# A gated mix of dilated local attention and a feed-forward layer: where the second parity's pipeline of logits and mixes begins

## The chip, the cores and the metric

The kernel runs on one core of a Trainium2 chip. The metric is the device time of one execution in microseconds; a profiled execution also has a span, from its first to its last instruction.

## The reference

Two layers share the input `x` (2048 tokens of 512 channels, float32) and are mixed by a gate per token:

```python
qkv = x @ wqkv                                  # 32 heads of 16 channels
idx = pos[:, None] - 2 * arange(8)[None, :]     # 8 keys, two tokens apart, back in time
logits = einsum(q, k[idx]) * 16 ** -0.5         # -1e9 where idx < 0
a = einsum(softmax(logits), v[idx]) @ wo
b = (gelu(x @ w_gate) * (x @ w_up)) @ w_down    # 1792 hidden channels
g = sigmoid((x * gate_w).sum(-1, keepdims=True))
return g * a + (1 - g) * b
```

A token looks only at tokens of its own parity, so even and odd tokens are two independent halves.

## The kernel before, in words

The two halves ("parities", 0 and 1) are worked one after the other. For each parity TensorE makes keys and queries (`keys`, and two last products in `key_one`), then values and the gate (`values`), and then the feed-forward layer in `ffn(par)`: 14 groups `f` of 128 hidden channels, each with seven products of gate and up weights (`gate_up`, L781 in `product`) and, from `f` = 2 on, pieces of the down projection (`down`, L830). All matrix products are split in a high and a low half of each operand and summed (three matmuls for one), and the gate, up and value products are combined from sums and differences of blocks, so that seven block products do the work of eight. VectorE and ScalarE make the sums, the halves (the low half of a hidden block is L801), the GELU and the copies out of the accumulators. The halves of the weights come partly from memory again (`ws`) and partly through an accumulating DMA of GpSimd (L740).

Attention runs beside that on VectorE. It is cut in eight *units*, four per parity (128 channels, so 8 heads, each). For a unit there are:

- `load_kq`: three DMAs on SyncE's queue for keys (L523, L524) and queries (L520) into a tile `kq` that exists once.
- `scores` (the logits): four times a product of 128 x 2048 elements (L539) and a sum over the 16 channels of a head (L542), and a mask for the first tokens (L546).
- `exps`: maximum (L553) and subtraction (L555) on VectorE, exponential on ScalarE (L557, with a load of the function's table ahead of it).
- `shares`: sum (L562), reciprocal (L564), for the second parity the product with the gate (L566), and the product with the exponentials (L568).
- `load_values`: two DMAs (L523, L524) into a tile `v` that exists once.
- `mix`: four times a product (L585) and three halving sums (L589, L591, L593), and after every second of them a transposition (L598) and four DMAs on SyncE's queue that store it (L600, `os`).

The logits of a unit live in one of two tiles `lg`; the product of L539 and of L585 goes to one tile `prod`.

A generator, `attention`, writes these steps in one order. The code of the matrix products calls `pull` with a budget at many places; each step of the generator has a price, and as many steps are emitted there as the budget buys. L539 and L585 (`paced`) are also tied to the last matmul emitted by then, and so can't start before it. All steps are emitted at a lower priority than the work around them. A planner with a simulated timeline then lays down each engine's own order; VectorE, ScalarE, SyncE and GpSimd work theirs in that order. At the very end `need_o` emits what is left of a unit before `finish` reads its stored result (L1040), halves it (L90, L91) and multiplies it with `wo` (L1062).

The loop of the generator over the units, `i` from 0 to 7 (unit 4 is the second parity's first), cut to what the change touches:

```python
            if i not in ready:
                if i >= PIPE and keyed(i + 1):
                    load_kq(*units[i + 1])
                yield from exps(*un)
            ...
            pipe, ahead = i >= PIPE and keyed(i + 1), i and keyed(i + 1)
            if not pipe and ahead:
                load_kq(*units[i + 1])
            load_values(*un)
            if pipe:
                yield from logits(i + 1)
                ...
                yield from exps(*units[i + 1])
            ...
            yield from mix(*un)
            ...
            elif ahead:
                yield from logits(i + 1)
```

`keyed(i)` says that the keys and queries of unit `i` have been emitted; `logits` is `scores`, with `load_kq` ahead of it if that wasn't done yet. With `pipe`, the shares of unit `i + 1` follow the mix of unit `i`.

Of the kernel before, what the change touches and what calls it, by code (L numbers as in the profile page):

```python
# [33 lines left out]
LOAD = 4.0  # L34


PIPE = 4
BT = 4
MASKED = -1e9 * DH ** 0.5
LOWS = (4, 8, 10), (4, 6, 8, 10, 12)  # L40
# [8 lines left out]
def tile_gated_mix(ctx: ExitStack, tc: tile.TileContext, xt, wqkv, wff, wo, out):  # L49
# [458 lines left out]
    def load_kq(par, u):  # L508
        hh, c = divmod(u, 2)
        kq = KQ.pop() if KQ else pool.tile([P, 3 * NP - 1, UC], F32, name="kq")  # L510
        k, q = kq[:, :2 * NP - 1], kq[:, 2 * NP - 1:]
        LG[par, u] = k, q
        if not (par or u):

            nc.gpsimd.memset(k[:1, :NP - 1], 0.0)
            for a, b in (1, P - 15), (P - 15, P):
                nc.sync.dma_start(k[a:b, :NP - 1], k[a - 1:b - 1, NP:])
            return
        load_slots(k, KS[par, hh][c], paced)
        paced(nc.sync.dma_start(q, QS[par, hh][c].rearrange("(p j) d -> p j d", j=NP)))  # L520
# [38 lines left out]
    def shares(par, u):  # L559
        lg = LG[par, u]  # L560
        m = pool.tile([P, UH, NP], F32, name="m")
        nc.vector.tensor_reduce(m, lg, axis=AX.X, op=OP.add)  # L562
        yield 0.7
        nc.vector.reciprocal(m, m)  # L564
        if par:
            nc.vector.tensor_tensor(m, m, g[:, par, None, :].to_broadcast([P, UH, NP]), op=OP.mult)  # L566
        yield 0.4
        nc.vector.tensor_tensor(lg, lg, m[:, :, :, None].to_broadcast([P, UH, NP, W]), op=OP.mult)  # L568
        yield 0.7
# [52 lines left out]
    def attention():  # L622
# [3 lines left out]
        def keyed(i):  # L626
            return i < len(units) and (units[i][0], units[i][1] // 2 * 2) in done
# [12 lines left out]
        for i, un in enumerate(units):  # L640
# [4 lines left out]
# [4 lines that stand above are left out]
            yield from need(un[0], 1)  # L649
            if i not in shared:  # L650
                yield from shares(*un)
            pipe, ahead = i >= PIPE and keyed(i + 1), i and keyed(i + 1)
            if not pipe and ahead:
# [702 lines left out]
```

## Time and profile before

| | |
|---|---|
| median of 3 runs | 593.22 us (592.76 to 597.3) |
| profiled execution | 592.89 us, span 591.1 us |
| TensorE busy | 585.7 us (99% of the span), clock 1.00 |
| VectorE busy | 535.0 us (91%) |
| ScalarE busy | 425.3 us (72%) |
| GpSimd busy | 126.8 us (21%) |
| HBM, over the span | 197 GB/s |

Busy time of an engine is the time in which one of its instructions ran. In the groups of instructions, a row gives line, engine, operation, what is written and read, and how often; in the timeline a row gives start and length in microseconds, and in brackets how long the engine sat idle before it and what ended that. In the list of waits a row gives the total, the count and the longest. A name with q behind the engine (SPq) is its queue of DMA issues. The second parity's keys are made from about 276 us on, its values follow, and its feed-forward runs from about 330 to 533 us.

### The profile page before, as it was taken

Reading aid. Unit: us, or ns where it says so; the run is one execution under the profiler, and the core shown is the slowest. Engines: PE = TensorE matmul, PEld = TensorE weight load, DVE = VectorE, ACT = ScalarE, POOL = GpSimd, SP = SyncE. Lnnn points to the kernel's source line nnn. Section 1 sums busy time; section 2 is a strip of 40 time slices with the busy share of each in tenths; the row PEclk is TensorE's granted clock in tenths of the full one; section 3 lists DMA queues with packets and bytes.
Section 4 is the critical chain, followed back from the end, with each engine's and each line's share of the span. In section 5 each row is a group of like instructions: output and inputs, shape, how many; then the busy total and the mean of one; then the engine's idle time right before and its main releaser. Section 6 shows DMA issues by size and latency. Waiting matters only on the chain.

```text
span 591.1 us, 8266 instructions
## 1 busy us (share of the span) xinstructions
PE 585.7 (99%) x2743; PEld 489.1 (83%) x2743; DVE 535.0 (91%) x628; ACT 425.3 (72%) x752; POOL 126.8 (21%) x153
## 2 busy tenths in 40 slices
PE   9999999999999999999999999999999999999997
PEld 7889888888888888888889888888888888887885
DVE  6989998999899995998997999998999899989882
ACT  6778667778887779786687655768776967796522
POOL 0140751112111212113120761112121212112200
PEclk9999999999999999999999999999999999999999
DMA  8789999978987979899989999969798989548915
GB/s 305 228 247 281 301 310 231 296 197 238 289 222 218 273 205 273 224 264 347 284 231 380 222 272 269 277 162 257 178 263 224 254 213 247 144 111 227 202 44 178
DMA packets 87848, 141.71 MB, mean 240 GB/s; under 512 B 8575, under 2 KB 49919, under 8 KB 87806
## 3 DMA queue, kind: packets, MB, share of 16 engines
q1 hardware_dynamic: 65454, 103.21, 52.2%
q0 software_dynamic: 22064, 37.59, 34.6%
q8 instruction: 21, 0.34, 0.2%
q10 hardware_dynamic: 288, 0.39, 0.2%
q14 instruction: 21, 0.17, 0.1%
HBM read 69.83 MB, written 46.49 MB: 197 GB/s over the span
## 4 chain that ended last, share of the span: by engine, by line
PE 96%; ACT 2%; DMA 1%; issue 0%; SPq 0%; DVE 0%; ACTq 0%
PE p L781 44%; PE p L830 13%; PE acc L830 12%; PE acc L478 11%; PE p L1062 6%; PE p L364 4%; PE acc L364 3%; PE p L478 2%; PE acc L1062 2%; DMA raw<-xt 1%; ACT A L90 0%; ACT L898 0%; ACT g L135 0%; ACT hl L805 0%; ACT hh L807 0%
## 5 line engine op out<-in xcount | busy, mean ns | idle before, releaser
L781 PE MATMUL p<-S,g 128*128 128x512 f32 x672 | 167.0, 389 | 0.0
L781 PEld LDWEIGHTS p<-S,g 128*128 128x128 f32 x672 | 125.8, 188 | 25.8
L781 PE MATMUL p<-A,g 128*128 128x512 f32 x504 | 125.8, 389 | 0.0
L781 PEld LDWEIGHTS p<-A,g 128*128 128x128 f32 x504 | 94.4, 188 | 19.8 <-ACT rt L845 0.4
L585 DVE TENSOR_TENSOR prod<-v,lg 128x2048 f32<-128x2048 f32 x32 | 72.8, 2274 | 1.4 <-DMA v<-vs 1.2
L542 DVE TENSOR_REDUCE lg<-prod 128x128 f32<-128x2048 f32 x32 | 73.0, 2280 | 0.2
L539 DVE TENSOR_TENSOR prod<-kq 128x2048 f32<-128x2048 f32 x32 | 72.9, 2277 | 0.2
L830 PE MATMUL p<-d,hh 128*128 128x512 f32 x224 | 68.6, 390 | 0.3 <-ACT p L824 0.3
L830 PE MATMUL acc<-d,hh 128*128 128x512 f32 x224 | 59.7, 389 | 0.0
L740 POOL DMA_DIRECT2D g<-raw x26 | 23.6, 907 | 161.1 <-ACT g L737 103.6
L792 ACT ACTIVATE c<-p 128x512 f32<-128x512 f32 x56 | 33.4, 597 | 33.7 <-PE p L781 33.6
L830 PEld LDWEIGHTS p<-d,hh 128*128 128x128 f32 x224 | 41.9, 188 | 9.5 <-ACT p L824 0.8
L830 PEld LDWEIGHTS acc<-d,hh 128*128 128x128 f32 x224 | 42.0, 188 | 8.7
L793 DVE TENSOR_TENSOR c<-c,s 128x512 f32<-128x512 f32 x56 | 37.8, 681 | 5.5 <-ACT c L792 5.2
L830 PE MATMUL p<-d,hl 128*128 128x512 f32 x112 | 42.1, 389 | 0.0
L797 DVE TENSOR_TENSOR c<-c 128x512 f32<-128x512 f32 x56 | 38.1, 683 | 1.3 <-ACT c L898 1.2
L589 DVE TENSOR_TENSOR prod<-prod 128x1024 f32<-128x1024 f32 x32 | 39.0, 1217 | 0.1
L845 ACT ACTIVATE rt<-p 128x512 f32<-128x512 f32 x48 | 27.8, 596 | 15.0 <-PE p L830 14.8
L786 ACT ACTIVATE s<-p 128x512 f32<-128x512 f32 x56 | 33.2, 594 | 5.3 <-PE p L781 4.9
L478 PE MATMUL acc<-d,S 128*128 128x512 f32 x144 | 35.5, 390 | 0.1
L830 PE MATMUL acc<-d,hl 128*128 128x512 f32 x112 | 35.1, 389 | 0.0
L772 POOL DMA_DIRECT2D d<-r x23 | 19.8, 860 | 68.9 <-ACT d L771 41.6
(222 smaller groups left out, 1062.3 us busy)
## 6 DMA issues: line engine op xcount, KB each, us to landing
g<-raw POOLq DMA_DIRECT2D x26, 512.0 KB, 6.7
ws<-g SPq DMA_DIRECT2D x14, 768.0 KB, 5.9
g<-ws SPq DMA_DIRECT2D x14, 768.0 KB, 6.7
r<-wff SPq DMA_DIRECT2D x28, 256.0 KB, 4.4
raw<-wff SPq DMA_DIRECT2D x14, 512.0 KB, 4.6
d<-r POOLq DMA_DIRECT2D x23, 256.0 KB, 6.7
ws<-raw SPq DMA_DIRECT2D x14, 384.0 KB, 5.8
raw<-ws SPq DMA_DIRECT2D x14, 384.0 KB, 4.0
```

The costliest lines, as they stand in the source:

```text
L364: LAST[:] = [nc.tensor.matmul(ps[:, :n], x[:, ts], VO[b][w][:, kc * WQ:kc * WQ + n], start=first, stop=(kc == 1 and i == 2), skip_group_ch ...
L478: LAST[:] = [nc.tensor.matmul(ps, x[:, ts], w, start=(start and kc == i == 0), stop=(kc == 1 and i == 2), skip_group_check=True)]
L539: paced(nc.vector.tensor_tensor(prod, spans(k, jj), q[:, jj:jj + 2, None, :].to_broadcast([P, 2, W, UC]), op=OP.mult))
L542: nc.vector.tensor_reduce(two_of(lg, jj), prod.rearrange("p j w (h d) -> p (j w) h d", d=DH), axis=AX.X, op=OP.add)
L585: paced(nc.vector.tensor_tensor(prod.rearrange("p j w (h d) -> p (j w) h d", d=DH), spans(v, jj).rearrange("p j w (h d) -> p j w h d", d=D ...
L589: nc.vector.tensor_tensor(prod[:, :, :4], prod[:, :, :4], prod[:, :, 4:], op=OP.add)
L781: LAST[:] = [nc.tensor.matmul(ps, w_, a_, start=(start and kc == 0 and n == 0), stop=(kc == 1 and n == 2), skip_group_check=True)]
L792: nc.scalar.activation(c, ps, AF.Copy)
L793: nc.vector.tensor_tensor(c, c, s, op=OP.add)
L797: nc.vector.tensor_tensor(ge, ge, up, op=OP.mult)
L830: LAST[:] = [nc.tensor.matmul(pp, a[:, ts], w, start=(i == 0 and n == 0 and gr == 0), stop=(i == 1 and n == 2), skip_group_check=True)]
L1062: LAST[:] = [nc.tensor.matmul(pa, a, b, start=(first and n == 0), stop=(last and n == 2), skip_group_check=True)]
```

## The change

One constant goes from 4 to 5. It is read at the two places quoted above only.

```diff
-PIPE = 4
+PIPE = 5
```

For units 5 and later nothing changes in the generator. For unit 4 the condition `i >= PIPE` is now false. So its `exps` are not preceded by `load_kq` of unit 5; that load follows unit 4's `shares`, ahead of `load_values`. The logits and the exponentials of unit 5 no longer stand between unit 4's shares and its mix: the mix comes first, then unit 5's logits. Unit 6's keys and queries are loaded, and unit 5's exponentials and shares emitted, at the head of the next turn of the loop. The order of steps goes from

logits 4, exps 4, shares 4, logits 5, exps 5, mix 4, shares 5, logits 6, ...

to

logits 4, exps 4, shares 4, mix 4, logits 5, exps 5, shares 5, logits 6, ...

and the steps from logits 6 on stand as before.

## The prediction

> **What bounds the kernel now.** I read the head of the page first, then what TensorE waits for, then what VectorE waits for, and last the timelines of VectorE, SyncE and ScalarE in the stretch that the edit reorders.
>
> ```profile
> span 591.1 us, 8266 instructions
> PE 585.7 (99%) x2743; PEld 489.1 (83%) x2743; DVE 535.0 (91%) x628; ACT 425.3 (72%) x752; POOL 126.8 (21%) x153
> PEclk9999999999999999999999999999999999999999
> PE 96%; ACT 2%; DMA 1%; issue 0%; SPq 0%; DVE 0%; ACTq 0%
> PE p L76 <- DVE warm L73: 1.0, 1, 1.0
> PE p L830 <- ACT p L824: 0.3, 1, 0.3
> DVE m L562 <- ACT lg L557: 15.3, 7, 4.1
> DVE c L793 <- ACT c L792: 5.2, 8, 1.4
> DVE prod L585 <- DMA v<-vs: 1.2, 1, 1.2
> ```
>
> TensorE is busy for 585.7 of 591.1 us at the full granted clock, is 96% of the chain that ended last, and waits for nothing but 1.0 us at the start and 0.3 us once. Nearly all of the 5.4 us in which it is idle is lead-in and the tail behind the last matmul. So a reordering of attention work on VectorE can hardly gain: at most the 0.3 us, and nothing of the matmuls, whose number stays the same. It can lose as soon as it makes TensorE wait. The question is therefore how much slack each of VectorE's products for TensorE has, and what the edit takes from it.
>
> **The stretch that is reordered.** Write S for a unit's logits (L539 and L542, four pairs), E for its exponentials (L553, L555 on VectorE, then L557 on ScalarE), H for its shares (L562 to L568), M for its mix (L585 to L598), and number the units 0 to 7; unit 4 is the second parity's first. These rows of the timeline (start, length, engine, line) are what the present order S4 E4 (H4) S5 (E5) M4 (H5) S6 leaves:
>
> ```profile
> 342.33 0.38 SPq L523 DMA_DIRECT2D v<-vs  x1
> 367.01 2.29 DVE L539 TENSOR_TENSOR prod<-kq 128x2048 f32<-128x2048 f32 x1
> 369.32 0.32 SPq L523 DMA_DIRECT2D kq<-ks  x1
> 376.28 0.68 DVE L555 TENSOR_TENSOR lg<-lg,m 128x512 f32<-128x512 f32 x1
> 376.50 1.28 ACT L557 ACT_TABLE_LOAD   x1
> 376.88 2.29 DVE L539 TENSOR_TENSOR prod<-kq 128x2048 f32<-128x2048 f32 x1
> 377.79 0.63 ACT L557 ACTIVATE lg<-lg 128x512 f32<-128x512 f32 x1
> 379.08 0.68 DVE L562 TENSOR_REDUCE m<-lg 128x64 f32<-128x512 f32 x1
> 382.47 0.55 DVE L564 RECIPROCAL m<-m 128x64 f32<-128x64 f32 x1
> 386.28 0.22 DVE L566 TENSOR_TENSOR m<-m,g 128x64 f32<-128x64 f32 x1
> 389.21 0.68 DVE L568 TENSOR_TENSOR lg<-lg,m 128x512 f32<-128x512 f32 x1
> 399.68 0.33 SPq L523 DMA_DIRECT2D kq<-ks  x1
> 403.67 2.27 DVE L585 TENSOR_TENSOR prod<-v,lg 128x2048 f32<-128x2048 f32 x1
> 411.55 0.69 DVE L562 TENSOR_REDUCE m<-lg 128x64 f32<-128x512 f32 x1 [2.22 <-ACT lg L557]
> 421.30 3.81 SPq L600 DMA_DIRECT2D os<-tb  x4
> 430.19 0.82 SPq L523 DMA_DIRECT2D v<-vs  x1
> 433.72 2.25 DVE L539 TENSOR_TENSOR prod<-kq 128x2048 f32<-128x2048 f32 x1
> 433.83 2.93 SPq L600 DMA_DIRECT2D os<-tb  x4
> ```
>
> The reader is to see three things. First, between L555 of unit 4 (ends 376.96) and L562 (379.08) stands the first logits instruction of unit 5: it covers unit 4's exponential. Unit 5's exponential, met within unit 4's mix, is not covered: L562 waits 2.22 us. Second, unit 4's values were already requested at 342.33, at once when unit 3's mix had read its last, and 61 us before the mix that uses them: loads go out when their buffer is free, not where the source puts them. Third, unit 5's keys go out at 369.32, when unit 4's last L539 ends, and the first S5 runs at 376.88 with no wait.
>
> **The change part by part.** No instruction, byte or matmul is added or removed. The order becomes S4 E4 H4 M4 S5 E5 H5 S6, and from S6 on it is the old one. Both orders spend the same budget ahead of S6, so the matmuls to which S6 and all later work are tied are the same.
>
> *Unit 4's exponential loses its cover.* The mix needs the shares, so nothing of the attention can stand between L555 and L562. Exposed: 377.79 + 0.63 = 378.42, minus 376.96, is 1.46 us of idle VectorE. Bounds: 0, if the product work of the feed-forward (0.6 us apiece) fills it, and 4.1, the longest such wait in the waits above. I take 1.5, as this very exponential was timed.
>
> The Trainium skill, "ScalarE: Activation LUTs", section "What ACT_TABLE_LOAD costs", charges a switch of tables with 1.28 us of load and a further 1.38 us of drain. The load has that length here, but the exponential starts at 377.79, 0.01 us behind it, so the second part does not appear behind the load; by the page's full figure this exposure would be an estimated 2.8 us in place of 1.5.
>
> *Unit 5's exponential gains a cover.* Unit 6's first logits now follow H5, as unit 5's followed H4, so the 2.22 us wait goes in full if unit 6's keys are there. Bounds: −2.2 to 0. I take −2.2, from the like case at 376.88.
>
> *The mix comes earlier, its values are there.* Unit 4's shares come out at about 378.4 + 0.68 + 0.55 + 0.22 + 0.68 = 380.6, and up to 2 us later with feed-forward work between. The values were asked for 38 us before that (342.33). Cost 0; the load of unit 5's values moves from 430.19 to about 410, ahead of S5, and is wanted only by M5.
>
> *The keys of units 5 and 6.* Unit 5's keys wait longer for their use: 0. Unit 6's lose their lead: requested at 399.68 for use at 433.72 so far, they can now go out only when S5's last L539 ends, as unit 5's did.
>
> ```profile
> L520 SPq DMA_DIRECT2D kq<-qs x7: 319/424/669, 102.3 to 456.3; - x7
> DMA to landing us min/median/max: 3.0/5.8/11.4
> ```
>
> Unit 5's had 376.88 − 369.32 = 7.6 us and were in time. The three issues, 0.3 to 0.4 us each, take some 1.3 us with their gaps, and the landing 5.8 in the middle, 11.4 at the longest: a wait of 0 at the median (7.1 against 7.6) and 1.3 + 11.4 − 7.6 = 5.1 at the worst. I take 0.
>
> *The eight stores of unit 4's result* move with it on SyncE. They follow M4's first L585 by 17.6 and 30.2 us (421.30 and 433.83 less 403.67), so from a start near 382 they go out near 400 and 412, in front of the loads of raw weights. One of those loads, with what waits for it:
>
> ```profile
> 396.64 0.44 SPq L760 DMA_DIRECT2D raw<-wff  x1
> 402.44 1.06 ACT L737 ACTIVATE g<-raw 128x1024 fp32r<-128x1024 f32 x1
> 403.79 0.86 POOL L740 DMA_DIRECT2D g<-raw  x1 [1.10 <-DMA kq<-ks]
> 411.90 1.05 ACT L742 ACTIVATE g<-raw 128x1024 fp32r<-128x1024 f32 x1
> 419.20 1.52 PE L781 MATMUL p<-A,g 128*128 128x512 f32 x6
> raw<-wff SPq DMA_DIRECT2D x14, 128.0 KB, 4.0
> ```
>
> 396.64 + 4.0 leaves 1.8 us to L737, and from the end of L742 (412.95) to the next product of its group, which by the order of the code reads these weights, another 6.2: an estimated 8 us of slack against 3.8 us of stores. Cost 0; without that cover it would be at most the 3.81 of one group of stores.
>
> *The sum.* VectorE: +1.5 − 2.2 = −0.7 us at S6, bounds −2.2 and +4.1 + 5.1 = +9.2. What reaches TensorE depends on two covers. The low halves of the feed-forward's products:
>
> ```profile
> 392.62 0.68 DVE L801 TENSOR_TENSOR hl<-c,hh 128x512 fp32r<-128x512 f32 x1
> 397.44 0.39 PE L830 MATMUL p<-d,hl 128*128 128x512 f32 x1
> ```
>
> By the order of the code the second row is the first matmul that needs the first: ready at 393.30, read at 397.44, 4.1 us of slack. And the tail, from the last mix to the last channels:
>
> ```profile
> 552.49 2.29 DVE L585 TENSOR_TENSOR prod<-v,lg 128x2048 f32<-128x2048 f32 x1 [1.25 <-DMA v<-vs]
> 582.53 0.69 DVE L91 TENSOR_TENSOR hl<-raw,hh 128x512 fp32r<-128x512 f32 x1 [6.62 <-ACT hh L90]
> 584.86 0.39 PE L1062 MATMUL p<-S,hl 128*128 128x512 f32 x1
> ```
>
> Ready at 583.22, read at 584.86: 1.6 us. The net of −0.7, or even +1.5 if unit 5's wait stays, passes neither. TensorE's path: 0. The profiled execution took 592.89 us, 0.33 below the median of 593.22; 592.89 + 0 + 0.33 gives a forecast of **593.2 us**, with its own range from −0.3 (the one wait of TensorE gone) to +2 (a VectorE slip of 3.6 against the tail's 1.6): 592.9 to 595.2.
>
> **The rivals.**
>
> *Late keys reach the tail.* If unit 6's keys land near their worst and unit 4's exponential is exposed, VectorE is 1.5 + 5.1 = 6.6 us behind at S6. It has 5.2 us of waits for L792 over the whole kernel, of which perhaps 1.5 fall behind S6 and could swallow part. 6.6 − 1.5 − 1.6 = 3.5 us: 596.7, between 595.2 and 598.2. For it: VectorE is 91% busy, and a chain of loads and mixes runs to the end (1.25 us of wait for values already). Against it: unit 5's keys, in the same place, were in time.
>
> *Slower by over 1%: low halves too late.* VectorE works its queue in order, and all orders are written before the run by a planner that lays out the whole program anew. If the low halves (L801) are put behind a unit-4 share or mix instruction that waits for the exponential, they are late by up to 4.1 (the longest wait) + 2.3 (one L585) = 6.4 us, against 4.1 of slack: 2.3 us of idle TensorE each time. It decides from 4.1 us on. The moved mix and what it displaces take some 30 us (403.67 to 433.72) and a feed-forward group 15 (14 of them in 330 to 533), so two to three groups are exposed; with three it is 3 × 2.3 = 6.9: 600.1 us. For it: a program with no slack on TensorE shows each new wait in full. Against it: no such half holds TensorE up so far, with an exposed exponential of 2.22 us in the same stretch. The Trainium skill, "TensorE: Matmul & The Clock Gate", section "What's actually happening", says that an idle window of some 3.4 us halves the clock; no row here shows it (the clock is full in all slices), and by it one gap of that length would add an estimated 1.7 us more.
>
> *Faster.* Without the 0.3 us wait and with the 1.25 us wait for values gone at no other loss, 593.2 − 1.5 = 591.7. Against it: the order from S6 on is unchanged, and that second wait already hides in the tail's slack. No row offers a gain of 1%, 5.9 us, which is more than all of TensorE's idle time.
>
> **How the numbers follow.** Forecast 0.58; late keys 0.13; a little faster 0.04; slower by over 1% 0.23; a gain of over 1% that no row explains 0.02. A change of 1% is about what a measurement of this kernel can tell from none; within it lie the first three, 0.75. The fourth is as large as it is because the planner's new order can't be seen from here and every step of it can only lose. The range reaches from the faster rival, 591.6, into the slower one, 599.6, which leaves out about 2 in 10.
>
> **What would show it.** Right: the first L585 of unit 4 at 380 to 384, S5 from about 411, unit 6's keys requested near 430, S6 within 2 us of 433.7; L562 of unit 4 waits some 1.5 us and that of unit 5 next to none; TensorE's waits stay at 1.3 us in all. Wrong: a wait of TensorE on L801, L800 or ScalarE's weight halves between 380 and 440, L539 waiting for keys at S6, or the last low half (L91) coming later than 1.6 us before its matmul.

## The result, and the profile after

The changed kernel takes 601.16 us (median of 6 runs, 598.22 to 604.72) against 593.23 us before; the ratio is 1.0135, with a 95% interval of 1.0107 to 1.0163. It is slower by some 8 us; its six runs span 6.5 us, those of the kernel before 5.4. The profiled execution took 604.72 us, the longest of the six, so the account below is of an execution 3.6 us above the median.

The head of the page after, with TensorE's waits and the main ones of VectorE (total, count, longest):

```profile
span 603.0 us, 8261 instructions
PE 590.3 (98%) x2743; PEld 492.0 (82%) x2743; DVE 536.4 (89%) x628; ACT 426.5 (71%) x752; POOL 126.8 (21%) x153
PEclk9999999999999999999999999999999899999997
PE 88%; issue 3%; DMA 3%; ACT 2%; DVE 2%; SPq 0%; POOL 0%; POOLq 0%; DVEq 0%; ACTq 0%
PE p L1062 <- ACT hh L90: 3.5, 1, 3.5
PE acc L830 <- DMA hl<-c: 2.9, 1, 2.9
PE p L1062 <- ACT c L792: 1.1, 1, 1.1
DVE prod L585 <- DMA v<-vs: 4.3, 1, 4.3
DVE prod L539 <- DMA kq<-qs: 3.1, 1, 3.1
```

The work is the same: 2743 matmuls, 628 instructions of VectorE. Beside the 1.0 us at the start that both have, TensorE waited 0.3 us before. Now it waits in the three rows above, 7.5 us in all, and for 0.4 us ahead of the reordered stretch. Its idle time, the span less the busy time, grows from 5.4 to 12.7 us, and its busy time by 4.6 us, nearly all of that in two stretches at a lower clock: 7.3 + 4.6 is the 11.9 us by which the span grew. The chain that ended last, 96% TensorE before, now passes through VectorE, DMAs and issue.

The reordered stretch in the timeline after (start, length, engine, line, and the idle time before):

```profile
378.61 0.69 DVE L562 TENSOR_REDUCE m<-lg 128x64 f32<-128x512 f32 x1 [1.49 <-ACT lg L557]
381.39 2.28 DVE L585 TENSOR_TENSOR prod<-v,lg 128x2048 f32<-128x2048 f32 x1
406.74 2.25 DVE L539 TENSOR_TENSOR prod<-kq 128x2048 f32<-128x2048 f32 x1
426.01 2.29 DVE L539 TENSOR_TENSOR prod<-kq 128x2048 f32<-128x2048 f32 x1
428.84 0.37 SPq L523 DMA_DIRECT2D kq<-ks  x1
434.33 0.69 DVE L555 TENSOR_TENSOR lg<-lg,m 128x512 f32<-128x512 f32 x1
438.18 2.29 DVE L539 TENSOR_TENSOR prod<-kq 128x2048 f32<-128x2048 f32 x1 [3.15 <-DMA kq<-qs]
440.38 0.68 DVE L562 TENSOR_REDUCE m<-lg 128x64 f32<-128x512 f32 x1
449.91 0.68 DVE L568 TENSOR_TENSOR lg<-lg,m 128x512 f32<-128x512 f32 x1
```

The order is the one announced. Unit 4's exponential is uncovered (1.49 us), its mix starts at 381.4, unit 5's logits at 406.7, and unit 5's exponential is covered. But the keys and queries of unit 6, asked for at 428.84, hold VectorE up for 3.15 us: unit 6's logits start at 438.18, 4.5 us later than before (433.72). That start understates the lag. Unit 5's shares, 2.1 us of work in four instructions (L562 to L568), were finished ahead of unit 6's logits before and now lie among them. At the first product of unit 5's mix both orders have the same work of the attention behind them. Unit 5's last share and that product before, and the same product after:

```profile
418.43 0.69 DVE L568 TENSOR_TENSOR lg<-lg,m 128x512 f32<-128x512 f32 x1
457.51 2.27 DVE L585 TENSOR_TENSOR prod<-v,lg 128x2048 f32<-128x2048 f32 x1
...
463.38 2.27 DVE L585 TENSOR_TENSOR prod<-v,lg 128x2048 f32<-128x2048 f32 x1
```

There the lag is 5.9 us.

The middle of TensorE's loss. The low half of a hidden block goes from VectorE (L797) over GpSimd's accumulating DMA (L806) to TensorE (L830); the first two rows are from the timeline before, the others from after:

```profile
459.22 0.86 POOL L806 DMA_DIRECT2D hl<-c  x1 [8.40 <-ACT hl L805]
467.25 0.84 PE L830 MATMUL acc<-d,hl 128*128 128x512 f32 x3
...
462.31 0.69 DVE L797 TENSOR_TENSOR c<-c 128x512 f32<-128x512 f32 x1
463.95 0.86 POOL L806 DMA_DIRECT2D hl<-c  x1 [11.14 <-ACT hl L805]
471.86 1.19 PE L830 MATMUL acc<-d,hl 128*128 128x512 f32 x4 [2.94 <-DMA hl<-c]
```

Before, 8.0 us lay between the issue and the matmul that reads the result. After, VectorE's product comes out late, the issue is 4.7 us later, the DMA takes 7.9 us (5.0 to 6.2 us for this group before), and TensorE stands for 2.94 us.

The tail, from unit 6's last product over unit 7's values to the last channels:

```profile
554.25 2.29 DVE L585 TENSOR_TENSOR prod<-v,lg 128x2048 f32<-128x2048 f32 x1
556.57 0.34 SPq L523 DMA_DIRECT2D v<-vs  x1
564.06 2.29 DVE L585 TENSOR_TENSOR prod<-v,lg 128x2048 f32<-128x2048 f32 x1 [4.32 <-DMA v<-vs]
585.77 0.71 DVE L598 STREAM_TRANSPOSE tb<-o 128x512 f32<-128x512 f32 x1
593.76 1.22 PE L1062 MATMUL p<-S,hh 128*128 128x512 f32 x2 [3.46 <-ACT hh L90]
```

Unit 7's values can go out only when unit 6's last product has left the one tile of values, and VectorE has nothing else left to do: 4.32 us of wait against 1.25 before. TensorE then waits for the channels made from the last transposition.

### The profile page after: what moved, and what is told of

Its sections match the earlier page's. It is cut to its first block, busy times and chain, and to the rows that moved or that the text cites. A ratio compares the mean times of both kernels' runs of the same rounds, so it can differ in the third digit from the quotient of the medians.

```text
span 603.0 us, 8261 instructions
## 1 busy us (share of the span) xinstructions
PE 590.3 (98%) x2743; PEld 492.0 (82%) x2743; DVE 536.4 (89%) x628; ACT 426.5 (71%) x752; POOL 126.8 (21%) x153
## 4 chain that ended last, share of the span: by engine, by line
PE 88%; issue 3%; DMA 3%; ACT 2%; DVE 2%; SPq 0%; POOL 0%; POOLq 0%; DVEq 0%; ACTq 0%
PE p L781 41%; PE p L830 12%; PE acc L830 11%; PE acc L478 10%; PE p L1062 5%; PE p L364 3%; PE acc L364 3%; PE p L478 2%; DMA hl<-c 1%; DMA raw<-xt 1%; DVE prod L589 1%; DVE prod L585 1%; DMA raw<-os 0%; DVE hl L91 0%; DMA os<-tb 0%
## 5 line engine op out<-in xcount | busy, mean ns | idle before, releaser
L585 DVE TENSOR_TENSOR prod<-v,lg 128x2048 f32<-128x2048 f32 x32 | 72.9, 2277 | 4.7 <-DMA v<-vs 4.3
L539 DVE TENSOR_TENSOR prod<-kq 128x2048 f32<-128x2048 f32 x32 | 72.8, 2276 | 3.3 <-DMA kq<-qs 3.1
L830 PE MATMUL p<-d,hh 128*128 128x512 f32 x224 | 68.8, 391 | 0.0
L830 PE MATMUL acc<-d,hh 128*128 128x512 f32 x224 | 59.7, 389 | 0.0
L830 PEld LDWEIGHTS p<-d,hh 128*128 128x128 f32 x224 | 42.3, 189 | 8.9
L830 PEld LDWEIGHTS acc<-d,hh 128*128 128x128 f32 x224 | 42.1, 188 | 8.7
L830 PE MATMUL p<-d,hl 128*128 128x512 f32 x112 | 42.6, 393 | 0.0
L797 DVE TENSOR_TENSOR c<-c 128x512 f32<-128x512 f32 x56 | 38.2, 684 | 3.7 <-ACT c L898 3.7
L830 PE MATMUL acc<-d,hl 128*128 128x512 f32 x112 | 35.4, 390 | 2.9 <-DMA hl<-c 2.9
L845 ACT ACTIVATE rt<-p 128x512 f32<-128x512 f32 x48 | 27.9, 595 | 11.9 <-PE p L830 11.2
```

Of the source, the lines that this page charges most:

```text
L539: paced(nc.vector.tensor_tensor(prod, spans(k, jj), q[:, jj:jj + 2, None, :].to_broadcast([P, 2, W, UC]), op=OP.mult))
L585: paced(nc.vector.tensor_tensor(prod.rearrange("p j w (h d) -> p (j w) h d", d=DH), spans(v, jj).rearrange("p j w (h d) -> p j w h d", d=D ...
L797: nc.vector.tensor_tensor(ge, ge, up, op=OP.mult)
L830: LAST[:] = [nc.tensor.matmul(pp, a[:, ts], w, start=(i == 0 and n == 0 and gr == 0), stop=(i == 1 and n == 2), skip_group_check=True)]
```

## The experiments

Two theories at the start. **Theory 1**: the late keys of unit 6 are the whole loss. **Theory 2**: the mix ahead of the logits costs by itself, through the uncovered exponential and what moves with it. Ratios are against the kernel before, run on the same chip. An edit that adds lines shifts the line numbers behind it: L590 of the next profile is the product that was L585.

**Unit 6 without its own keys, and the control.** In both orders, `load_kq` of unit 6 hands out unit 5's tile:

```diff
     def load_kq(par, u):
+        if (par, u) == (1, 2):
+            LG[par, u] = SAME[0]     # the keys and queries of unit 5
+            return
```

> The new order, but unit 6's logits are made from unit 5's keys and queries, which lie in the tile already: three DMAs less (1.4 MB) and no wait for them; the output of unit 6's heads is not the reference's. Theory 1 (the late keys of unit 6 are the whole loss): VectorE has no wait of 3.1 us at unit 6's first logits, TensorE's waits in the middle and at the tail go, and the time is that of before, 592.5 to 595. Theory 2 (the mix ahead of the logits costs by itself, through the uncovered exponential and the moved stores and loads): at least half of the 8 us stays, 597 to 603.

> The old order with unit 6's logits made from unit 5's keys and queries (output of unit 6's heads not the reference's): the control for the run above. Both theories: those keys came 30 us ahead of their use, so nothing changes, 592.5 to 594; a gain here would have to be taken off the other run's.

New order: 597.83 us, ratio 1.0063 (1.0042 to 1.0085). Old order: 593.61 us, 0.9986 (0.9967 to 1.0005). The control holds. Without the late keys the middle wait is gone, but about half of the loss stays: each theory is right for a part. What stays is at the tail (waits of TensorE, then of VectorE; the last row is the first product of unit 5's mix):

```profile
PE p L1067 <- ACT hh L90: 2.3, 1, 2.3
PE p L1067 <- ACT c L797: 0.8, 1, 0.8
DVE prod L590 <- DMA v<-vs: 3.9, 1, 3.9
...
459.86 2.27 DVE L590 TENSOR_TENSOR prod<-v,lg 128x2048 f32<-128x2048 f32 x1
```

Unit 6's logits start at 433.46 here, no later than in the old order, and still unit 5's mix starts 2.4 us late and the last transposition 4.8 us late. Unit 5's maximum, subtraction and shares, 3.4 us of work, were finished ahead of unit 6's logits in the old order and lie among them here; that is enough for the first of the two.

**The pipeline begun later still, or never.** `PIPE = 6` and `PIPE = 8`.

> The constant at 6: units 4 and 5 are worked without the pipeline, and it begins at unit 6, so the keys of unit 7 are asked for when unit 6's logits end and wanted one exponential later. Theory 1: the wait for keys moves to unit 7's first logits (2 to 4 us), unit 6's are in time, and the loss stays of the same kind, nearer to the tail: 596 to 604. Theory 2: two mixes stand ahead of the next logits, two exponentials are uncovered: more than with 5, over 603.

> The constant at 8: no pipeline in the second parity at all. Each unit's mix stands between the request for the next keys and the logits that read them, so no keys are late; all four exponentials are uncovered. Theory 1: near before, 592.5 to 596 (four uncovered exponentials of 1.5 us are within the slack or cost a little at the tail). Theory 2: the worst of all, over 605.

With 6: 602.77 us, 1.0146 (1.0128 to 1.0164). With 8: 604.27 us, 1.0172 (1.0154 to 1.0191). The row of TensorE's main wait in either, 6 first, and VectorE's wait for keys with 6:

```profile
PE p L1062 <- ACT hh L90: 7.3, 1, 7.3
DVE prod L539 <- DMA kq<-qs: 2.8, 1, 2.8
...
PE p L1062 <- ACT hh L90: 9.2, 1, 9.2
```

With 6 the wait for keys moves to unit 7 as expected. With 8 no keys are late, and the loss is the largest of the four settings: theory 1 is wrong as a whole. As these rows read, the pipeline's worth is that a unit's exponential and shares are done ahead of time; without it the last unit's logits, exponential and mix stand in one row at the end.

**The late keys alone, in the old order.** A first try only emits unit 6's load behind unit 4's mix:

```diff
-                if keyed(i + 2):
+                if keyed(i + 2) and i != 4:
                     load_kq(*units[i + 2])
 ...
+            if pipe and i == 4:
+                load_kq(*units[6])
```

> The old order, with one thing changed: unit 6's keys and queries are asked for behind unit 4's mix instead of 30 us earlier, so that they land after S6 is due. VectorE should wait 3 to 6 us at unit 6's first logits. Theory 1 (a wait of VectorE there is carried to TensorE, in the middle through a late low half and at the tail): slower by 4 to 9 us, 597 to 603. Theory 2 (the loss belongs to the order of mix and logits): within 2 us of before, 593 to 595.

593.34 us, 1.0006 (0.9972 to 1.0040), and no wait for unit 6's keys: the load went out at 414.83, in the middle of unit 4's mix. The edit did not do what it was for. It shows that the generator's emission runs well ahead of VectorE here, and so that the ties of L539 and L585 to matmuls don't hold VectorE up at this place. A second try ties the load's DMAs to unit 4's last L585 by a semaphore.

> The old order, with the load of unit 6's keys and queries tied to the end of unit 4's last product of the mix (near 429.7), where the new order's load also went out, since the run before this did not make them late. VectorE should wait 3 to 6 us at unit 6's first logits. If the late keys cost by themselves: 597 to 602. If their lag alone is hidden and only adds to the lag of the order: 593.5 to 596.

```profile
379.29 2.29 DVE L546 TENSOR_TENSOR prod<-kq 128x2048 f32<-128x2048 f32 x1 [2.20 <-DMA kq<-qs]
430.23 0.44 SPq L530 DMA_DIRECT2D kq<-ks  x1
440.99 2.29 DVE L546 TENSOR_TENSOR prod<-kq 128x2048 f32<-128x2048 f32 x1 [7.07 <-DMA kq<-qs]
PE p L1073 <- ACT hh L90: 2.7, 1, 2.7
```

599.51 us, 1.0107 (1.0060 to 1.0154). The load took until 440.99, longer than expected, and the old order with late keys loses 6 us (with a wait twice as long as in the new order). The first row is a wait of 2.20 us for unit 5's keys, on which the edit has no bearing.

**The uncovered exponential alone, in the old order.** Unit 5's first L539 is put behind unit 4's L568:

```diff
+            if (par, u, jj) == (1, 1, 0):
+                behind(ins.ins, SHARED[0].ins.name)   # unit 4's shares
```

> The old order, but unit 5's first logits instruction is held behind unit 4's shares, so nothing covers unit 4's exponential: the other suspect by itself. VectorE idles some 1.5 us near 378. Theory 1: lost in the slack, 593 to 594.5. Theory 2 (uncovered exponential carried to the tail): half of what stayed without the late keys (4.2 us), so 595 to 598.

596.48 us, 1.0053 (1.0022 to 1.0085): some 3 us, between 1.3 and 5.0. The run doesn't show the exposed 1.5 us alone. In its profile the four shares of unit 4 stand ahead of unit 5's logits, VectorE waits 1.49 us for unit 4's exponential, and the 2.22 us for unit 5's exponential are gone. Unit 6's logits start only 0.8 us late, unit 5's mix 3.1 us, with 1.5 us more of waits for copies and halves of the feed-forward in between. So the second theory holds for the order of the steps; how much of it is the exponential stays open.

**Unit 7 without its own values.** `load_values` of unit 7 hands out unit 6's tile; in the new order, without and with the keys of unit 6.

> The new order, but unit 7's mix reads unit 6's values, which lie in the tile already (the output of unit 7's heads is not the reference's): the wait of 4.3 us for values at unit 7's mix goes. Theory 1 with the tail (the lag is made longer by the single tile of values): 4 us and the tail's slower clock less, 595 to 598, with TensorE's wait in the middle still there. If the tail were not the place, 600 to 602.

> The new order with both left out: unit 6's logits from unit 5's keys, unit 7's mix from unit 6's values (their heads' output not the reference's). If the two waits for loads are all of the loss: 592.5 to 594.5, TensorE waiting for nothing. If the order costs besides: 595 to 598.

595.14 us, 1.0028 (0.9993 to 1.0062), and 595.30 us, 1.0017 (0.9984 to 1.0049). The first is 6 us faster than the change, with the keys still late (3.0 us of wait in its profile) and 0.9 us of TensorE's middle wait: without unit 7's load, most of what the order and the late keys cost is gone. In both runs the difference to before is not resolved.

**A second place for unit 7's values**, the tile of the keys and queries, which is free by then; nothing is left out:

```diff
-        VT[par, u] = v = pool.tile([P, 2 * NP - 1, UC], F32, name="v")
+        if (par, u) == (1, 3):
+            v = pool.tile([P, 3 * NP - 1, UC], F32, name="kq")[:, :2 * NP - 1]
+        else:
+            v = pool.tile([P, 2 * NP - 1, UC], F32, name="v")
+        VT[par, u] = v
```

> The old order, with unit 7's values loaded into the tile of the keys and queries, which is free after unit 7's logits, so that they don't wait for unit 6's mix to leave the tile of values (nothing left out). The wait of 1.2 us at unit 7's first product of the mix goes; TensorE did not wait for it: 592.5 to 594. Control for the next run.

> The new order with the same second place for unit 7's values. If the single tile of values at the tail is where the lag turns into time: 594 to 596.5, as with the values left out (595.1), TensorE's wait at the tail under 1 us. If not: 599 to 603.

Old order: 594.22 us, 1.0023 (0.9986 to 1.0059): no gain, TensorE had not waited there. New order: 597.65 us, 1.0059 (1.0028 to 1.0090), with runs from 594.7 to 602.4. The tail's wait is 0.5 us in its profile, but that execution took 602.4 us and lost its time in the middle:

```profile
PE acc L834 <- DMA hl<-c: 3.8, 1, 3.8
PE p L1066 <- ACT hh L90: 0.5, 1, 0.5
```

So tail and middle are two separate outlets. That the middle one makes the spread is not shown: the old order with the same edit ran from 592.6 to 600.8.

**The middle wait alone.** Group 8's low halves by VectorE instead of GpSimd's DMA (`LOWS` of the second parity without the 8), in the new order with and without the second place for the values:

> The new order with unit 7's values in the tile of the keys, and besides the low halves of hidden group 8 (of the second parity) made by VectorE instead of GpSimd's accumulating DMA, at 1.4 us more of VectorE's work. If the wait in the middle is that DMA's round trip behind a late VectorE, it goes, and with it the spread of the run before (594.7 to 602.4): 594 to 597, TensorE's waits under 2 us besides the start's. If the middle wait has another source, it stays at 1 to 4 us and the spread too.

> The new order with only the low halves of group 8 made by VectorE: the middle wait by itself taken out of the measured change. If middle and tail each hold about half of the loss of 8 us: 597 to 600, the tail's wait as it was (3 to 6 us, a lag grown by 1.4 us).  If the tail is nearly all of it: 600 to 604.

599.09 us, 1.0083 (1.0057 to 1.0109), and 600.40 us, 1.0107 (1.0077 to 1.0138). In both the middle wait is gone, and the four runs of each lie close together (598.2 to 599.2, and 600.0 to 600.7). The first expectation was missed: the time is no lower than with the middle wait, and VectorE's added work came out at the tail (TensorE waits 3.2 us there although no values are waited for). The second run lies just beyond the range for two equal halves, in the one for a tail that holds nearly all, with 3.9 us of TensorE's wait there.

**A lag of known size.** Unit 6's first L539 done twice or three times, in the old order:

```diff
+            for _ in range(3 if (par, u, jj) == (1, 2, 0) else 1):
                 paced(nc.vector.tensor_tensor(prod, spans(k, jj), ...
```

> The old order with the first product of unit 6's logits done twice (2.3 us more of VectorE, same result), for the size of its slack. Two of them cost 10 us. If the slack is the tail's 1.6 us and what lies beyond it grows with the wait for values and the slower clock: 595 to 599. If there is a step between 2.3 and 4.6 us: 593 to 594.5.

> The old order with the first product of unit 6's logits done three times (4.6 us more of VectorE, same result): a lag of known size at the place where the keys are late. If VectorE's lag of some 4.5 us is what costs, by whatever cause: 597 to 602, TensorE waiting at the tail (values of unit 7 waited for by 3 us or more). If VectorE has slack behind it: under 595.

2.3 us more: 599.46 us (599.05 without the one run at 606.48), 1.0082 (1.0052 to 1.0112). 4.6 us more: 604.03 us, 1.0165 (1.0127 to 1.0203). The second profile's waits:

```profile
PE p L1063 <- ACT hh L90: 7.2, 1, 7.2
DVE prod L586 <- DMA v<-vs: 5.8, 1, 5.8
```

By the ratios the added 2.3 us cost 4.9 us (3.1 to 6.7) and the added 4.6 us cost 9.8 (7.5 to 12.1): about twice their length, in the old order and with unit 6's keys in time. That points to one cause, VectorE's lag, whatever makes it. In ten of the profiled executions, the start of the last transposition (L598) and the time:

| kernel | last transposition | time | difference |
|---|---|---|---|
| before | 575.2 | 592.9 | 17.7 |
| both loads left out | 577.7 | 594.9 | 17.2 |
| uncovered exponential | 579.0 | 595.7 | 16.7 |
| new order, unit 5's keys for unit 6 | 580.0 | 597.8 | 17.8 |
| one more product | 580.4 | 596.8 | 16.4 |
| late keys, old order | 581.9 | 598.8 | 16.9 |
| `PIPE = 6` | 583.7 | 602.6 | 18.9 |
| two more products | 584.3 | 603.2 | 18.9 |
| after | 585.8 | 604.7 | 18.9 |
| `PIPE = 8` | 586.3 | 604.1 | 17.8 |

The time is the start of VectorE's last instruction for the attention plus 16.4 to 18.9 us; in the other seven profiled executions it is 17.0 to 18.8 us. Late waits of TensorE move both columns alike, so the table doesn't tell which engine held the other up; the waits above do.

## Why the prediction was wrong, point by point

*What bounds the kernel.* TensorE's 99% was read rightly, and so was that nothing could be gained. Two steps failed. In the sum, unit 6's keys were put at 0 and cost a wait of 3.15 us, most of the way from the −0.7 us at S6 to the +4.5 measured. And from there to TensorE, a lag within +1.5 us "passes neither" cover, at a price of 0; the runs showed a lag of 5.9 us at unit 5's mix that left through both covers and cost 8 us. Only the slack of TensorE's inputs was asked for, and VectorE has little to give back. Its row for 435 to 540 us of the kernel before (busy time and, in brackets, instructions):

```profile
435.00:540.00 105.00, 104.67 (x463) 86.31 (x462) 98.99 (x103) 81.62 (x138) 17.80 (x22) 1.00 0.79 212
```

99.0 of 105 us are busy. Of the 6.0 us of idle time 3.1 are waits for two exponentials, which a lag doesn't shorten. After, unit 6's logits start 4.5 us late and unit 6's last product 10.2 us late; 5.7 of these are TensorE's own first two waits and its slow stretch (2.9 + 1.1 + 1.7), so the lag against TensorE is 4.5 us, as at the start. The page's 91% had that in it, but the prediction used it only as a point for a rival.

*"Both orders spend the same budget ahead of S6, so the matmuls to which S6 and all later work are tied are the same".* True, but of no use: the load that went out at 414.83 showed that these ties don't bind.

*Unit 4's exponential, 1.5 us.* Measured 1.49, so the size was right. Its price was 0 by the sum; the order that exposes it costs some 3 us in the old kernel, with the reservation made there.

*Unit 5's exponential, −2.2 us.* That wait went, but the gain was not kept. From unit 4's mask (L546) to unit 6's first product, VectorE idles 3.8 us before and 7.6 after: +1.5 and −2.2 as forecast, +3.2 for keys, and 1.3 more in waits for the feed-forward's copies. The term "−0.7 at S6" was +4.5. The mark itself was ill chosen: the cover found for unit 5's exponential, unit 6's first product, puts 2.1 us of unit 5's shares behind it, which the sum left out.

*"I take 0" for unit 6's keys.* The mis-sized term. The prediction set the middle landing of 5.8 us against the 7.6 us that unit 5's keys had. After, unit 5's logits have fewer feed-forward instructions behind their last L539: from 428.84 to the end of L555 at 435.02 are 6.2 us, and the load took 9.3. It was late in each profile of the new order that reads them, by 2.0 to 4.0 us, within the stated bound of 5.1. The precedent was luck, too. Unit 5's keys, whose 7.6 us were enough in the profile before, were late in four other profiles of the old order, by 0.4 to 2.2 us; the edits of these have no bearing on that load. One of them, the first try above:

```profile
378.38 2.29 DVE L539 TENSOR_TENSOR prod<-kq 128x2048 f32<-128x2048 f32 x1 [1.22 <-DMA kq<-qs]
```

*The values are there, the stores have slack.* Neither unit 4's values nor the moved stores were waited for. The other end of the same tile, unit 7's values, was named only as a point for a rival, and is the place where most of the time went.

*The cover of low halves, 4.1 us.* The row chosen was a half made by VectorE itself. Five of the second parity's 14 groups (`LOWS`) go over GpSimd's DMA, whose round trip leaves less: 8.0 us from issue to matmul before, less 5.0 to 6.2 us of landing there, is 2 to 3 us.

*The tail's 1.6 us* is not contradicted as a bound, but wrong as a price: the added lags above cost about twice their length, the wait for values and the lower clock included.

*The rivals.* "Late keys reach the tail" named the place and the wait; its 596.7 was too low, as it let 1.5 us be swallowed behind S6 and took the rest of the lag at its length. "Slower by over 1%" gave 600.1 us, next to the 601.2 measured, by luck: its mechanism, a low half that comes too late, is one of the two outlets; but it occurs once, not three times, at 471 and not beside the moved mix, and its cause is the other rival's. The two were one rival: late keys and an uncovered exponential make a lag, and it leaves through a low half and through the tail. The range ended at 599.6, below the median. The prediction's own sign of being wrong, L539 waiting for keys at S6, came true.

## What to carry to other kernels

Where the bounding engine waits for nothing, look next at how busy the engine is that feeds it: one at 94% over the last hundred microseconds hands a lag on to the end, so an added 2.3 us there is a cost and not a detail behind a cover. To price a reordering, compare at a place where both orders have done the same work. When a step moves ahead, ask of each tile that exists once what the move does to the next load into it; here the keys' load lost a lead of 30 us, and the tile of values at the end turned the lag into time. For a load that must land within a given gap take the long end of its landings, not the middle, and for a cover take the row with the least slack, the one with a DMA in it.

## What the runs showed of the hardware that was not expected

The clock of TensorE can fall after a short gap. Stretches of the windows view (stretch, length, busy time of PE, PEld, DVE, ACT and POOL, granted clock, DMA share, GB/s), behind the gaps of 2.94 and 3.46 us after, and behind the 2.3 us of the new order with unit 5's keys:

```profile
475.00:477.20 2.20, 2.20 (x7) 1.72 (x6) 1.88 (x4) 0.60 (x1) 0.00 (x0) 0.59 0.82 254
597.00:599.20 2.20, 2.20 (x6) 1.24 (x4) 0.42 (x1) 0.60 (x1) 0.00 (x0) 0.50 0.58 223
588.00:590.00 2.00, 2.00 (x6) 1.57 (x5) 0.09 (x1) 0.60 (x1) 0.00 (x0) 0.50 0.00 0
```

The clock is halved or nearly so. Two other gaps left it at 1.00: one of 2.04 us (one more product) and one of 2.66 us (late keys tied, old order; 1.00 from 589.8 to 594 us). So the length of the gap alone doesn't decide: after 2.28 us the clock fell, after 2.66 us it did not. After every gap of 2.94 us or more in these profiles it fell to 0.50. The stretch of 473 to 477.2 at 0.59 costs 1.7 us, the last 5.3 us at 0.50 another 2.6. The Trainium skill, "TensorE: Matmul & The Clock Gate", section "What's actually happening", has the half clock after an idle window of about 3.4 us. Here it also came behind gaps of 2.28 and 2.94 us.

Open remains why unit 6's keys took 8.2 to 10.8 us from the first request to the product that waited for them, and how the loss divides from run to run between the middle and the tail; the runs that remove one of them don't add up to the whole. Open, too, is the spread: of the 78 executions of the kernel before, nine took 596.5 to 600.3 us, and none of these was profiled.
